# Loading the first token tile whole from the ScalarE queue, and starting the sync queue with w1

## The chip, the cores and the metric

The kernel runs on one core of one Trainium2 chip. The metric is device time in microseconds (us) of one execution, as the median of several. A profile shows one execution, and times in it count from its first instruction. The profiled span is about 2.3 us shorter than the device time of the same execution (547.7 against 549.95 us for the kernel before). In profile lines PE is TensorE, PEld its weight loads, DVE VectorE, ACT ScalarE, POOL GpSimd and SP the sync engine; a q behind the name means the part of the engine that issues DMAs and waits. A load has landed when its completion counter says that all its data have arrived.

## The reference

The reference normalises 2048 tokens of 512 features, runs sliding-window attention with 32 query heads over the last 512 cached keys, runs an MLP on the same normalised tokens, and gates one with the other.

```python
x = A_x
xn = _layernorm(x, axis=-1)
s = _A_ref(xn, A_k_cache, A_v_cache, A_wq, A_wo)   # attention, then wo
g = _silu(_B_ref(xn, B_w1, B_w2))                  # h = silu(xn @ w1); h @ w2
return x + s * g
# x: 1x2048x512, w1: 512x1792, wq: 512x4096, all bf16
```

## The kernel before

The tokens are worked on in four blocks of 512 (four tiles of 128). Only the very start matters for this change. The first block of x and the weights of the MLP are loaded from two queues. `nc.sync` is the queue of the sync engine (SPq in the profile), `nc.scalar` that of ScalarE (ACTq).

```python
new_x(0)
x0v = x2[ds(0, BLK), :].rearrange("(j p) d -> p j d", p=P)
nc.sync.dma_start(x_blk[0][0:HP4, 0, :], x0v[0:HP4, 0, :])      # tile 0, rows 0-63
nc.scalar.dma_start(x_blk[0][HP4:P, 0, :], x0v[HP4:P, 0, :])    # tile 0, rows 64-127
nc.scalar.dma_start(x_blk[0][:, 1, :], x0v[:, 1, :])            # tile 1
NE = NEARLY * P
nc.sync.dma_start(w1_sb[0][:, :, 0 : NE // 2], ...)             # w1, first piece, 256 KB
nc.sync.dma_start(w1_sb[0][:, :, NE // 2 : NE], ...)            # w1, second piece, 256 KB
nc.scalar.dma_start(x_blk[0][:, 2:4, :], x0v[:, 2:4, :])        # tiles 2 and 3
nc.sync.dma_start(w1_sb[0][:, :, NE:], ...)                     # w1, third piece, 384 KB
nc.sync.dma_start(w1_sb[1][:, :, 0:NE], ...)                    # w1, fourth piece, 512 KB
# ... (the rest of w1, w2, later x blocks, keys, wq, values: all on nc.sync)
```

The compute that waits for these loads:

```python
stats(0, 0)                 # VectorE, tile 0
stats(0, 1)                 # VectorE, tile 1, in front of tile 0's centering
for j in range(2):
    rstd_first(j)           # ScalarE
    center(0, j)            # VectorE
warm_up(10)                 # TensorE: matmuls nobody reads
# ... tiles 0 and 1 are transposed on TensorE (t_ps) and copied into xnT
for i in range(2 * FH):
    h_pair(i, i // FH)      # TensorE: h_ps <- xnT (256 tokens) and w1
    if i == 3:
        # ... tiles 2 and 3 are transposed here
```

The last act of the kernel is the output's last pieces, each a store on the sync queue:

```python
for t in range(2):
    # ... last matmuls, two VectorE operations
    nc.sync.dma_start(out2[ds(base // HQ * BLK + (2 + t) * P, P), HALF:], xo)
```

The softmax here doesn't subtract the row's maximum and nothing guards it: scores larger than these inputs give would overflow.

## Time and profile before

| | before |
|---|---|
| median of 3 runs | 550.09 us (549.88 to 551.0) |
| span of the profiled execution | 547.7 us |
| TensorE busy | 542.2 us (99%) |
| first h matmul starts | 6.58 us |
| last matmul starts | 543.59 us |

The busy table of the page and its chain of waits say that TensorE is the limit:

```profile
PE 542.2 (99%) x2676; PEld 261.1 (48%) x2676; DVE 458.4 (84%) x1258; ACT 392.1 (72%) x1125; POOL 20.5 (4%) x41
...
PE 98%; DMA 1%; SPq 0%; DVE 0%; issue 0%
```

The timeline of the first 10 us has, in each line, start, duration, engine, source line, operation, what it writes and reads, and in brackets the idle time in front of it and what ended that:

```profile
0.73 0.55 ACTq L619 DMA_DIRECT2D x_119<-in_A_x_dram  x1
0.73 0.58 SPq L618 DMA_DIRECT2D x_119<-in_A_x_dram  x1
...
1.32 0.60 ACTq L620 DMA_DIRECT2D x_119<-in_A_x_dram  x1
1.37 0.81 SPq L622 DMA_DIRECT2D w_0_111<-in_B_w_dram  x1
...
3.29 0.69 DVE L109 BATCH_NORM_STATS2 st<-x_119 128x6 f32<-128x512 bf16 x1 [2.15 <-DMA x_119<-in_A_x_dram]
...
4.12 0.66 DVE L109 BATCH_NORM_STATS2 st<-x_119 128x6 f32<-128x512 bf16 x1
...
6.58 1.99 PE L691 MATMUL h_ps<-xnT_107,w_0_111 128*128 128x256 bf16 x16
...
8.72 1.48 PE L691 MATMUL h_ps<-xnT_107,w_0_111 128*128 128x256 bf16 x12 [0.16 <-DMA w_0_111<-in_B_w_dram]
...
10.23 0.33 PEld L691 LDWEIGHTS <-w_1_112 128*128 128x128 bf16 x4 [0.30 <-DMA w_1_112<-in_B_w_dram]
```

Read the two statistics first. Tile 0's (3.29) waits for a load; tile 1's (4.12) has no bracket, so tile 1 was there in time. TensorE then starts h at 6.58 and is held up twice by w1, at 8.72 and 10.23. The chain of waits of the same stretch (start, duration, what) names the third piece of w1:

```profile
2.78 5.90 DMA w_0_111<-in_B_w_dram
8.68 0.05 issue
8.72 1.48 PE h_ps L691 x12
```

From the completion counts of the DMAs in the trace come the landings: tile 0's halves 2.84 and 3.20, tile 1 3.79, w1's four pieces 6.32, 7.47, 8.68 and 10.18 us.

The table by stretches shows that the DMA engines were not full at this time; its last two columns are their busy share and GB/s (the share can read a little over 1):

```profile
3.50:4.00 0.50, 0.50 (x2) 0.15 (x1) 0.49 (x1) 0.21 (x1) 0.00 (x0) 1.00 0.41 98
4.00:4.50 0.50, 0.50 (x2) 0.15 (x1) 0.48 (x2) 0.26 (x1) 0.00 (x0) 1.00 0.58 162
```

The last matmul starts at 543.59, the last store is issued at 544.81, and the span ends at 547.68. In between, the sync engine works through a closing list of ten semaphore waits, eight of them one for each completion counter of the DMAs of its own and of ScalarE's queue. Two views, restricted to the sync engine, show it. First, what it waited for after 540 us (total, times, longest):

```profile
SPq L852 <- DMA out_dram<-x_t: 1.1, 1, 1.1
```

Second, its closing instructions between 546.365 and 546.85 us, that is from the landing of the last store on:

```profile
L852 SPq EVENT_SEMAPHORE  x8: 27/28/28, 546.4 to 546.8; - x8
```

So the third wait of the list is the one that waits 1.1 us for the last store. It ends at 546.37, and seven waits still come after it, one every 0.06 us, though nothing is left to wait for.

### The profile page before, as it was taken

The page shows a single profiled execution, that of the slowest core. Times are in us where ns is not written, and L with a number is a line of the kernel's source. Part 1 is how long each engine was busy: PE and PEld are TensorE (multiplying, and loading weights), DVE is VectorE, ACT ScalarE, POOL GpSimd, SP SyncE. Part 2 cuts the span into 40 slices and gives each one's busy share as a digit, 9 for nine tenths or more (in the row PEclk, how much of TensorE's full clock was granted, in tenths as well). Part 3 has the DMA queues.
Part 4 walks back from the last instruction along what each step waited for, and adds up shares of the span by engine and source line. Part 5 has one row for each costly group of instructions (what it writes and reads, how often), then busy time and mean ns, then how long its engine had stood idle before and what let it go on. Part 6 is the DMA issues. An engine that isn't in the chain of part 4 may idle for free.

```text
span 547.7 us, 8533 instructions
## 1 busy us (share of the span) xinstructions
PE 542.2 (99%) x2676; PEld 261.1 (48%) x2676; DVE 458.4 (84%) x1258; ACT 392.1 (72%) x1125; POOL 20.5 (4%) x41
## 2 busy tenths in 40 slices
PE   8999999999999999999999999999999999999997
PEld 5644444444444444444444444444444444444586
DVE  6888888887886788898889888988889889988897
ACT  5558757866875677777777777777788888888600
POOL 1000010000000000010001000100010000000010
PEclk9999999999999999999999999999999999999999
DMA  8969769778849799979887988798889778888921
GB/s 260 278 115 186 160 131 165 152 152 159 168 89 193 171 199 226 211 154 193 160 152 145 189 163 143 155 187 161 145 161 183 153 152 156 185 153 154 173 78 40
DMA packets 298909, 89.69 MB, mean 164 GB/s; under 512 B 282352, under 2 KB 297968, under 8 KB 298864
## 3 DMA queue, kind: packets, MB, share of 16 engines
q1 hardware_dynamic: 297056, 85.02, 79.2%
q0 software_dynamic: 1312, 3.67, 2.6%
q10 hardware_dynamic: 496, 0.46, 0.3%
q8 instruction: 21, 0.34, 0.2%
q14 instruction: 24, 0.20, 0.1%
HBM read 17.30 MB, written 2.10 MB: 35 GB/s over the span
## 4 chain that ended last, share of the span: by engine, by line
PE 98%; DMA 1%; SPq 0%; DVE 0%; issue 0%
PE o_ps L277 20%; PE q_ps L212 20%; PE sc_ps L234 20%; PE s_ps L335 15%; PE oB_ps L181 9%; PE h_ps L148 7%; PE m_ps L478 4%; PE h_ps L691 2%; DMA w_0_111<-in_B_w_dram 1%; SPq L622 0%; SPq L618 0%; SPq L623 0%; PE t_ps L658 0%; DVE m_4_6595 L502 0%; DVE x_t L604 0%
## 5 line engine op out<-in xcount | busy, mean ns | idle before, releaser
L237 ACT ACTIVATE p_all<-sc_ps 128x512 bf16<-128x512 f32 x512 | 305.1, 597 | 104.4 <-PE sc_ps L234 100.4
L249 DVE TENSOR_SCALAR p_all<-p_all,rden 128x512 bf16<-128x512 bf16 x512 | 158.0, 351 | 9.1
L283 DVE CAST oT<-o_ps 128x512 bf16<-128x512 f32 x128 | 88.2, 689 | 35.8 <-PE o_ps L277 35.0
L237 ACT ACTIVATION_READ_ACCUMULATOR p_all<-sc_ps 128x1 f32 x512 | 100.4, 196 | 0.0
L224 DVE CAST qT<-q_ps 128x512 bf16<-128x512 f32 x111 | 76.3, 687 | 3.3 <-PE q_ps L212 3.3
L234 PEld LDWEIGHTS <-qT 128*128 128x128 bf16 x512 | 50.1, 98 | 60.5 <-issue 0.2
L335 PEld LDWEIGHTS <-oT 128*128 128x128 bf16 x384 | 37.6, 98 | 45.3
L247 DVE RECIPROCAL rden<-den 128x2 f32<-128x2 f32 x256 | 40.5, 158 | 11.1 <-ACT p_all L237 10.9
L158 ACT ACTIVATE th<-h_ps 128x512 bf16<-128x512 f32 x42 | 25.0, 595 | 4.0 <-PE h_ps L148 3.9
L335 PE MATMUL s_ps<-wo_big_2344,oT 128*128 128x512 bf16 x84 | 26.0, 379 | 0.0
L335 PE MATMUL s_ps<-wo_big_2084,oT 128*128 128x512 bf16 x84 | 26.0, 379 | 0.0
L335 PE MATMUL s_ps<-wo_big_2345,oT 128*128 128x512 bf16 x84 | 26.0, 379 | 0.0
L335 PE MATMUL s_ps<-wo_big_2083,oT 128*128 128x512 bf16 x84 | 26.0, 379 | 0.0
L234 PE MATMUL sc_ps<-kT_91,qT 128*128 128x512 bf16 x64 | 24.3, 379 | 0.0
L234 PE MATMUL sc_ps<-kT_93,qT 128*128 128x512 bf16 x64 | 24.3, 379 | 0.0
L234 PE MATMUL sc_ps<-kT_95,qT 128*128 128x512 bf16 x64 | 24.3, 379 | 0.0
L234 PE MATMUL sc_ps<-kT_94,qT 128*128 128x512 bf16 x64 | 24.3, 379 | 0.0
L234 PE MATMUL sc_ps<-kT_96,qT 128*128 128x512 bf16 x64 | 24.3, 379 | 0.0
L234 PE MATMUL sc_ps<-kT_97,qT 128*128 128x512 bf16 x64 | 24.3, 379 | 0.0
L234 PE MATMUL sc_ps<-kT_92,qT 128*128 128x512 bf16 x64 | 24.3, 379 | 0.0
L234 PE MATMUL sc_ps<-kT_98,qT 128*128 128x512 bf16 x64 | 23.9, 379 | 0.0
L277 PE MATMUL o_ps<-pT,v_100 128*128 128x512 bf16 x64 | 18.4, 379 | 0.0
(316 smaller groups left out, 858.4 us busy)
## 6 DMA issues: line engine op xcount, KB each, us to landing
pT<-p_all SPq DMA_TRANSPOSE x128, 4.4
x_e<-in_A_x_dram POOLq DMA_DIRECT2D x12, 128.0 KB, 3.2
out_dram<-x_e POOLq DMA_DIRECT2D x12, 128.0 KB, 2.3
w_0_113<-in_B_w_dram SPq DMA_DIRECT2D x1, 896.0 KB, 8.9
w_1_114<-in_B_w_dram SPq DMA_DIRECT2D x1, 896.0 KB, 9.8
w_0_111<-in_B_w_dram SPq DMA_DIRECT2D x2, 256.0 KB, 5.1
w_1_112<-in_B_w_dram SPq DMA_DIRECT2D x1, 512.0 KB, 6.9
x_130<-in_A_x_dram SPq DMA_DIRECT2D x1, 512.0 KB, 8.8
```

What stands on the lines that cost most here:

```text
L148: nc.tensor.matmul(h_ps[:, lo : lo + n], w1_sb[f // FH][:, c, (f % FH) * P : (f % FH + 1) * P], xnT[b][:, c, lo : lo + n], start=(c == 0), ...
L158: nc.scalar.activation(th, h_ps, ACT.Tanh, scale=0.5)
L181: nc.tensor.matmul(cur["ps"], hT[b][f // 2][:, f % 2, j * P : (j + 1) * P], w2_sb[f // FH][:, f % FH, :], start=(f == 0), stop=(f == NFC - 1),
L212: nc.tensor.matmul(cur["ps"], wq_sb[h // REP][:, c, (h % REP) * DH : (h % REP + 1) * DH], xnT[b][:, c, :], start=(c == 0), stop=(c == ND - 1),
L224: nc.vector.tensor_copy(qT[s], cur["ps"])
L234: nc.tensor.matmul(sc, qT[s][:, j * P : (j + 1) * P], kT[h // REP], start=True, stop=True)
L237: nc.scalar.activation(p_all[s][:, :, j, :], sc.rearrange("p (kc q) -> p kc q", q=P), ACT.Exp, scale=INV_SQRT_DH, accum_out=den[s][:, j : ...
L247: nc.vector.reciprocal(rden, den[s][:, j0 : j1 + 1])
L249: nc.vector.tensor_scalar_mul(p_all[s][:, :, j, :], p_all[s][:, :, j, :], rden[:, j - j0 : j - j0 + 1])
L277: nc.tensor.matmul(cur["ps"], v_sb[h // REP][:, kc, :], pT[s][:, kc, :], start=(kc == 0), stop=(kc == NKC - 1))
L283: nc.vector.tensor_copy(oT[s // 2][:, s % 2, :], cur["ps"])
L335: nc.tensor.matmul(acc[j], oT[(b * HQ + h) // 2][:, h % 2, j * P : (j + 1) * P], wo_of(h), start=(h == 0), stop=(h == HQ - 1),)
```

## The change

The intent is to let the sync queue begin with w1, which TensorE is seen waiting for, and to load tile 0 with one load instead of two half ones. The diff has every changed line; context lines are left out:

```diff
@@ -52,7 +52,6 @@
     FH = NFC // 2
     HALF = BLK // 2
     HP = HQ // 2
-    HP4 = P // 2
 
@@ -615,8 +614,7 @@
         new_x(0)
         x0v = x2[ds(0, BLK), :].rearrange("(j p) d -> p j d", p=P)
-        nc.sync.dma_start(x_blk[0][0:HP4, 0, :], x0v[0:HP4, 0, :])
-        nc.scalar.dma_start(x_blk[0][HP4:P, 0, :], x0v[HP4:P, 0, :])
+        nc.scalar.dma_start(x_blk[0][:, 0, :], x0v[:, 0, :])
         nc.scalar.dma_start(x_blk[0][:, 1, :], x0v[:, 1, :])
         NE = NEARLY * P
         nc.sync.dma_start(w1_sb[0][:, :, 0 : NE // 2], w1v[:, :, 0 : NE // 2])
```

## The prediction

> What bounds it now. TensorE is busy 99% of the 547.7 us span (busy table) and is 98% of the chain of waits; granted clock 1.00. After about 11 us it has no gap that matters. So the change can only pay or cost in the first 11 us, and what it moves there passes nearly one to one to the end.
>
> Start-up before (timeline, and DMA completion events of the trace):
> - x tile 0's lower half (sync queue) and upper half (ScalarE queue) are issued at 0.73 us; the ScalarE half lands at 2.84, the sync half at 3.20. Statistics start at 3.29, transposes at 5.35, the last xnT copy ends near 6.55, the first h matmul starts at 6.58. Tile 1 lands at 3.79; VectorE takes it at 4.12 (0.3 us of slack).
> - w1's first piece is issued at 1.37, behind the half tile, and lands at 6.32; pieces two and three at 7.47 and 8.68, the first piece of w1's other half at 10.18. TensorE loses about 0.31 us at 8.72 and 0.18 us at 10.23: 0.5 us that w1 causes.
> - The DMA share by half microseconds is 0.41 and 0.58 from 3.5 to 4.5 us and over 1.0 (near 340 GB/s) only afterwards. An earlier w1 fills an idle hole.
>
> What the change does. It removes one issue from the sync queue: 0.58 us and a 0.06 us step, so w1 is issued 0.64 us earlier (0.73). The ScalarE queue keeps three issues, the first with 128 packets instead of 64. No compute instruction changes; bytes are the same. The Trainium skill ("DMA: Bandwidth & Descriptors", Rules for kernel authors) advises one 128-partition transfer instead of two to disjoint halves, as both use the same 16 engines; the trace agrees so far that the halves land 0.36 us apart, the sync queue's last.
>
> Costed:
> 1. x tile 0 whole on the ScalarE queue: first packet near 2.08, 8 packets of about 50 ns per engine, interleaved with w1's of 27 ns: about 0.65 us, plus 0.3 us to completion: 3.0 to 3.3 (estimate), as now. Tile 1 lands at 3.6 to 4.0. The x chain moves by -0.2 to +0.2 us; I take -0.05.
> 2. w1: first packet near 2.35 instead of 3.0. Landings 0.3 to 0.6 us earlier, less than 0.64 because x shares the engines and the stream is saturated from 4.5 us on.
> 3. TensorE's gaps of 0.31 and 0.18 us shrink: -0.35 us.
> 4. At 18.0 us the first q needs wq's first group, which lands at 17.6 and moves earlier with the stream: no new wait.
>
> Sum: about -0.4 us, 0.07%, below the scatter of the times (549.88 to 551.0).
>
> Predicted: 549.7 us, 8 in 10 between 549.1 and 550.7. Faster by over 2%: 0.003; within 2%: 0.994; slower by over 2%: 0.003.
>
> Right if the profile shows: w1's first issue at 0.73, landing near 5.8; statistics starting at 3.1 to 3.4; first h matmul within 0.2 us of 6.58; waits of the h weight loads for w1 down from 0.9 + 0.3 us to under 0.6; the q group of 18.1 starting near 17.7; everything after shifted, not changed.
>
> Wrong if: the 512 packets of w1's first piece, now beside x's, hold up tile 0 or 1 (a descriptor path shared by both queues would do it): then tile 1's statistics start after 4.3, h after 6.8, and the gain becomes a loss of up to 1 us. Or if tiles 2 and 3, which land at 6.60 just when VectorE wants them (6.62), come later: their transposes at 10.7 would hold TensorE. Or if w1 is limited by the memory and not by its issue: then nothing moves.

## The result and the profile after

| | before | after |
|---|---|---|
| median, 6 runs each | 550.04 us (549.84 to 551.0) | 549.6 us (549.49 to 549.63) |
| ratio of means, 95% interval | | 0.999 (0.9977 to 1.0002) |
| span of the profiled execution | 547.7 us | 547.3 us |
| w1's first piece lands | 6.32 us | 4.17 us |
| tile 1 lands | 3.79 us | 4.57 us |
| first h matmul starts | 6.58 us | 7.19 us |
| 29th h matmul starts (the first that reads w1's fourth piece) | 10.23 us | 10.24 us |
| last matmul starts | 543.59 us | 543.60 us |
| from there to the end (the tail) | 4.09 us | 3.66 us |

A ratio is the mean time of one kernel's fast runs over the mean of the other's in the same rounds, so it is not quite the ratio of the medians. The 0.44 us between the medians is 0.08%. The interval includes 1, because one run of before took 551.0; the six runs of each do not overlap (549.63 at most against 549.84 at least).

The predicted time, 549.7 us, was right to 0.1 us. The table says that the reason was not: TensorE's last matmul starts at the same time in both kernels, and the whole difference of the spans lies behind it. The page is otherwise unchanged:

```profile
PE 542.3 (99%) x2676; PEld 261.5 (48%) x2676; DVE 458.3 (84%) x1258; ACT 392.2 (72%) x1125; POOL 20.5 (4%) x41
...
PE 98%; DMA 1%; DVE 0%; ACTq 0%; ACT 0%; issue 0%
```

The timeline after, of the same stretch:

```profile
0.73 0.43 ACTq L617 DMA_DIRECT2D x_119<-in_A_x_dram  x1
0.73 0.45 SPq L620 DMA_DIRECT2D w_0_111<-in_B_w_dram  x1
...
1.19 0.46 ACTq L618 DMA_DIRECT2D x_119<-in_A_x_dram  x1
1.23 0.51 SPq L621 DMA_DIRECT2D w_0_111<-in_B_w_dram  x1
...
3.33 0.69 DVE L108 BATCH_NORM_STATS2 st<-x_119 128x6 f32<-128x512 bf16 x1 [2.18 <-DMA x_119<-in_A_x_dram]
...
4.59 0.69 DVE L108 BATCH_NORM_STATS2 st<-x_119 128x6 f32<-128x512 bf16 x1 [0.36 <-DMA x_119<-in_A_x_dram]
...
7.19 3.22 PE L689 MATMUL h_ps<-xnT_107,w_0_111 128*128 128x256 bf16 x28
...
10.24 0.60 PE L689 MATMUL h_ps<-xnT_107,w_1_112 128*128 128x256 bf16 x4
```

Tile 1's statistics now have a bracket: they wait for tile 1, although it was issued earlier than before (1.19 against 1.32). Everything behind them is late, and h starts 0.61 us later. But then 28 matmuls run in one piece: the waits for w1 are gone. The chain of waits names tile 1's load where it named w1's:

```profile
1.19 3.38 DMA x_119<-in_A_x_dram
4.57 0.02 issue
4.59 0.70 DVE st L108
...
7.19 3.65 PE h_ps L689 x32
```

The idle hole of the DMA engines is filled, as was hoped:

```profile
3.50:4.00 0.50, 0.50 (x3) 0.15 (x1) 0.50 (x1) 0.00 (x0) 0.00 (x0) 1.00 1.11 365
4.00:4.50 0.50, 0.50 (x2) 0.15 (x1) 0.20 (x2) 0.23 (x1) 0.00 (x0) 1.00 1.14 346
```

At the end, the same two views of the sync engine (the second from 546.365 to 546.43 us):

```profile
SPq L850 <- DMA out_dram<-x_t: 0.6, 1, 0.6
```

```profile
L850 SPq EVENT_SEMAPHORE  x1: 28/28/28, 546.4 to 546.4; - x1
```

The last store lands at the same time as before. But the wait for it is now the last of the list; the other nine were done while the store was still under way. Seven waits of 0.06 us are 0.43 us; the tail is shorter by 4.09 - 3.66 = 0.43 us, and the spans differ by 0.42.

Why the position moved can be read in the compiled programs. The loads and stores of the two hardware queues take eight completion counters in turn (they are called DMAHW0 to DMAHW7 there), and the closing list asks for them in the order of their numbers. Before a counter is taken again, its previous use is waited for, so the last store's line tells its counter:

```
before: DMACopy out_dram<-x_t 128x256 [waits DMAHW0_49,DVE_49]
after:  DMACopy out_dram<-x_t 128x256 [waits DMAHW7_49,DVE_49]
```

The change removes one load at the start. That shifts every later load and store by one counter, and the last one from the first counter to the last. The traces agree: the last store of before uses the same counter that the third closing wait asks for, that of after the counter of the tenth.

### The profile page after: what moved, and what is told of

It is laid out like the page before. It is cut to its first block, busy times and chain, and to the rows that moved or that the text cites. A ratio compares the mean times of both kernels' runs of the same rounds, so it can differ in the third digit from the quotient of the medians.

```text
span 547.3 us, 8530 instructions
## 1 busy us (share of the span) xinstructions
PE 542.3 (99%) x2676; PEld 261.5 (48%) x2676; DVE 458.3 (84%) x1258; ACT 392.2 (72%) x1125; POOL 20.5 (4%) x41
## 4 chain that ended last, share of the span: by engine, by line
PE 98%; DMA 1%; DVE 0%; ACTq 0%; ACT 0%; issue 0%
PE sc_ps L233 20%; PE q_ps L211 20%; PE o_ps L276 20%; PE s_ps L334 15%; PE oB_ps L180 9%; PE h_ps L147 7%; PE m_ps L477 4%; PE h_ps L689 2%; DMA x_119<-in_A_x_dram 1%; DVE st L108 0%; PE t_ps L647 0%; PE t_ps L656 0%; DVE m_4_6594 L501 0%; ACTq L617 0%; DVE x_t L603 0%; ACT xnT_107 L651 0%
## 5 line engine op out<-in xcount | busy, mean ns | idle before, releaser
L351 POOL DMA_DIRECT2D out_dram<-x_e x12 | 6.6, 550 | 314.7 <-DVE rden L246 258.4
```

## The experiments

Two questions were open. Does the gain come from the tail (theory T) or from w1's head start (theory S, my prediction)? And why did tile 1 come late, so that the start-up gained nothing?

Medians of before in these rounds: 550.08 us (11 or 12 runs, 549.71 to 552.27), and 550.13 in the last two experiments. The long runs of before pull its mean up, and with it the ratios down a little.

### The changed kernel, with the last store back on the first counter

```diff
         for s in range(NSTEP):
             b, h = divmod(s, HQ)
+            if s in (70,):
+                pad = const.tile([16, 16], BF16, name=f"pad{s}", tag=f"pad{s}")
+                nc.sync.dma_start(pad, x2[0:16, 0:16])
```

> The changed kernel with one 512-byte load more on the sync queue, in mid-kernel (step 70), so the sync and ScalarE queues issue as many DMAs as in the kernel before and the last output store uses the first of the eight completion counters again. Theory T (tail): the 0.44 us come from the closing waits of the sync engine alone; undone here: ratio to before 1.000 (550.0 us), seven waits of 0.06 us after the last store has landed, end 4.1 us after the last matmul begins; the start-up stays as in the changed kernel. Theory S (start-up, as predicted): the gain is w1's 0.64 us head start; it stays: 549.6 us, ratio 0.9992.

Measured: 549.92 us (549.73 to 550.25), ratio 0.9994 (0.9981 to 1.0006). The tail is back at 4.08 us; between the last store's landing and 547.15 us the sync engine has eight closing waits again, the one that waited and seven more:

```profile
L853 SPq EVENT_SEMAPHORE  x8: 28/28/28, 546.7 to 547.1; - x8
```

A 512-byte load in mid-kernel, which nothing reads, took back about 0.3 of the 0.44 us in the medians, and all of the tail in the trace. The start-up of this trace also differed from the changed kernel's first one: tiles 2 and 3 landed at 7.41 instead of 6.90 us, TensorE waited to transpose them, and the last matmul started at 543.89. So the time by itself speaks for T but not sharply; the tail does. The wait:

```profile
10.77 0.72 PE L656 MATMUL t_ps<-ident,x 128*128 128x128 bf16 x8 [0.24 <-DVE x L123]
```

### The kernel before, with the last store on the last counter

```diff
+            if s in (70, 71, 72, 73, 74, 75, 76):
+                pad = const.tile([16, 16], BF16, name=f"pad{s}", tag=f"pad{s}")
+                nc.sync.dma_start(pad, x2[0:16, 0:16])
```

> The kernel before with seven 512-byte loads more on the sync queue (steps 70 to 76), so that the last output store uses the last of the eight counters, as in the changed kernel. Start-up untouched. T: 0.42 us faster than before, 549.6 us, ratio 0.9992; one wait left after the last store has landed, end 3.66 us after the last matmul begins. S: no gain, ratio 1.000 or a little slower for the seven loads.

Measured: 549.55 us (549.48 to 550.03), ratio 0.9987 (0.9975 to 1.0). The tail is 3.66 us, the last matmul starts at 543.57, and the start-up is that of before (first h matmul 6.79, 29th 10.22). What the sync engine waited for, and its one closing wait after the landing (546.355 to 546.42 us):

```profile
SPq L855 <- DMA out_dram<-x_t: 0.6, 1, 0.6
```

```profile
L855 SPq EVENT_SEMAPHORE  x1: 28/28/28, 546.4 to 546.4; - x1
```

So the whole time of the changed kernel is had without the change, by seven useless loads. T holds and S falls. This run also isolates the start-up: with the same tail, the changed kernel (549.60, and 549.67 when repeated) is not faster than this kernel with before's start-up (549.55); the runs are of different rounds.

### w1 held back by one small load

The rest of the experiments ask about the start. The first one puts a small load in front of w1.

```diff
+        pad = const.tile([16, 16], BF16, name="pad")
+        nc.sync.dma_start(pad, x2[0:16, 0:16])
         nc.scalar.dma_start(x_blk[0][:, 0, :], x0v[:, 0, :])
         nc.scalar.dma_start(x_blk[0][:, 1, :], x0v[:, 1, :])
```

> The changed kernel with a 512-byte load as the first issue of the sync queue, so w1 is issued about 0.6 us later, near its old time, and x tile 0 stays whole on the ScalarE queue; as many DMAs as before. Theory C (w1's packets, now on the engines before tile 1's, hold tile 1 up by 0.8 us, and that loss takes back w1's gain): tile 1 lands before 4.2 us, the first h matmul starts near 6.6, and the h weight loads wait for w1 again; start-up as a whole as before, and with the tail of before 550.0 us, ratio 1.000. Rival (the 128-packet first tile itself delays tile 1 in its own queue): tile 1 still lands near 4.6 and h starts near 7.2, with w1 later too: 550.2 or more.

Measured: 550.09 us (549.93 to 550.57), ratio 0.9998 (0.9985 to 1.0012). The time is as theory C said, but its mechanism failed: tile 1 landed at 4.63, and h started at 7.14. The trace shows that the experiment was badly dosed. The small load's issue took 0.40 us, not the 0.6 that I had assumed from the half tile's, so w1 was issued at 1.19, 0.02 us after tile 1. The packets of the two were then sent mixed. It tells nothing between C and its rival, which names tile 0 in tile 1's own queue as the cause.

### Tile 1 at the head of the sync queue

```diff
-        nc.scalar.dma_start(x_blk[0][:, 1, :], x0v[:, 1, :])
+        nc.sync.dma_start(x_blk[0][:, 1, :], x0v[:, 1, :])
```

> The changed kernel with x tile 1 moved to the head of the sync queue, in front of w1; as many DMAs as in the changed kernel, so its tail. C: tiles 0 and 1 land by 3.4 us, the first h matmul starts near 6.5, w1's pieces land with less than 0.3 us of waits: 0.3 to 0.5 us faster than the changed kernel, near 549.2 us, ratio to before 0.9984. If w1 is limited by bytes ahead of it: its waits return, h starts at 6.5 but TensorE reaches the transposes at 10.7 as before: 549.6 us.

Measured: 549.26 us (549.0 to 549.87), ratio 0.9983 (0.997 to 0.9996). The timeline:

```profile
3.56 0.69 DVE L108 BATCH_NORM_STATS2 st<-x 128x6 f32<-128x512 bf16 x1 [2.42 <-DMA x<-in_A_x_dram]
...
4.38 0.66 DVE L108 BATCH_NORM_STATS2 st<-x 128x6 f32<-128x512 bf16 x1
...
6.84 3.71 PE L689 MATMUL h_ps<-xnT,w 128*128 128x256 bf16 x32
```

Tile 1 is no longer waited for. Tile 1 landed at 3.37 and tile 0 at 3.53, a little later than the 3.4 expected, and h started at 6.84, not 6.5. Tiles 2 and 3 landed at 5.47 instead of 6.90. But h then ran through 32 matmuls with hardly a wait for w1, and the last matmul started at 543.30 us, 0.30 earlier than in the changed kernel. In this trace the head start that was to be gained is there; one trace alone does not prove it, as a later section shows. With the tail of the changed kernel its median is below both.

### w1 held back by two small loads

```diff
+        for i in range(2):
+            pad = const.tile([16, 16], BF16, name=f"pad{i}", tag=f"pad{i}")
+            nc.sync.dma_start(pad, x2[0:16, 0:16])
         nc.scalar.dma_start(x_blk[0][:, 0, :], x0v[:, 0, :])
```

> The changed kernel with two 512-byte loads at the head of the sync queue (the earlier hold had one, and w1 was then issued 0.02 us after tile 1, too close to tell). w1's first piece is now issued near 1.6 us, clearly after tile 1 (near 1.2). Theory D (the loads of the two queues are turned into packets one whole load at a time, in the order of issue, so tile 1 waits for w1's 512 packets when w1 was issued first or at the same time): tile 1 lands by 3.9 us, its statistics follow tile 0's without a wait for the load, the first h matmul starts by 6.6. Rival (tile 1 waits for tile 0 in its own queue): tile 1 lands near 4.6 as in the changed kernel and h starts near 7.2. Tail by T: the last store uses the second counter, so one closing wait fewer than before comes after it: 4.03 us from the start of the last matmul to the end against 4.09.

Measured: 549.65 us (549.31 to 549.86), ratio 0.9987 (0.9973 to 1.0001).

```profile
1.17 0.46 ACTq L621 DMA_DIRECT2D x<-in_A_x_dram  x1
1.64 0.42 SPq L623 DMA_DIRECT2D w<-in_B_w_dram  x1
...
3.81 0.66 DVE L108 BATCH_NORM_STATS2 st<-x 128x6 f32<-128x512 bf16 x1
...
6.57 2.33 PE L692 MATMUL h_ps<-xnT,w 128*128 128x256 bf16 x17 [0.44 <-DMA w<-in_B_w_dram]
```

Tile 1, issued 0.02 us earlier than in the changed kernel and behind the same whole tile 0 in the same queue, landed at 3.38 instead of 4.57 us. Apart from the two small loads, only w1 had moved, to 1.64. So it is w1 in front of it, on the other queue, that holds tile 1 up, and the rival falls. The packets in the trace say how. Packets begun in each quarter of a microsecond (w1's are 512 bytes, the tiles' 1 KB):

```
                        2.25 2.50 2.75 3.00 3.25 3.50 3.75 4.00
after  ScalarE queue      34   47    7    0   13   75   39    1   (to 2.99: tile 0; from 3.25: tile 1)
after  sync queue, w1      1   34  134  169  145   34   94  169
two    ScalarE queue      84   53   53    2    1    1    6   17   (to 3.24: tiles 0, 1; then tiles 2 and 3)
loads  sync queue, w1      0    0   26   40   25    8   29   68
```

In the changed kernel the ScalarE queue falls silent between tile 0 and tile 1 while w1's first piece is sent, and the sync queue drops while tile 1 is sent. So these loads took turns nearly as wholes, in the order of issue: tile 1, 128 packets, stood behind w1's 512. This is not shown as a rule. In the first hold, with issues 0.02 us apart, the packets mixed. In the kernel before, tiles 2 and 3 were issued 0.58 us after w1's first piece, and yet 53 of their packets and 62 of w1's were begun in the quarter from 4.75 us. The counts add up all DMA engines, so whether a single engine took the loads in turn is not told.

The price is seen in the last line of the timeline: h now starts at 6.57 with a wait for w1, whose first piece landed only at 6.53. The last matmul started at 543.49. The tail was 4.04 us with the last store on the second counter, 0.05 less than on the first, where one wait of 0.06 was expected.

### Tile 0 split by columns instead of rows

In the kernel before, the first issues were long (0.55 to 0.60, and 0.81 for w1's first piece, against 0.43 to 0.46 after). This asks whether loads of 64 partitions make them so.

```diff
-        nc.sync.dma_start(x_blk[0][0:HP4, 0, :], x0v[0:HP4, 0, :])
-        nc.scalar.dma_start(x_blk[0][HP4:P, 0, :], x0v[HP4:P, 0, :])
+        DH2 = D // 2
+        nc.sync.dma_start(x_blk[0][:, 0, 0:DH2], x0v[:, 0, 0:DH2])
+        nc.scalar.dma_start(x_blk[0][:, 0, DH2:], x0v[:, 0, DH2:])
```

> The kernel before with tile 0 split by columns instead of rows: two loads of 128 partitions x 256 columns, one on each queue; the same bytes, as many DMAs, the same order. Theory H (loads of 64 partitions are what made the first issues of the kernel before long and w1's first piece slow): first issues under 0.5 us instead of 0.56 to 0.60, w1's first piece's issue under 0.55 instead of 0.81, and its landing before 5.4 instead of 6.32. Rival (any split over two queues costs it): issues stay near 0.6 and 0.8, w1's first piece lands after 6. Time between 549.6 and 550.3 in either case.

Measured: 550.24 us (549.94 to 552.09), ratio 1.0003 (0.9987 to 1.0019). The halves were issued in 0.39 and 0.41 us, w1's first piece in 0.42, and it landed at 5.17: theory H on all three. But its landing is not due to the shape alone: with 64-partition loads absent too, w1 landed at 6.53 in the experiment with two small loads, where it stood behind tile 1. Here w1 was issued 0.02 us after tile 1, the two were sent mixed as in the first hold, tile 1 landed at 4.89 and h started at 7.41. Tile 0 itself landed no later than before (2.83 and 2.99 against 2.84 and 3.20), so I put the late tile 1 down to the closer issue; no experiment tested that apart.

### The two kernels once more

> The changed kernel once more, unaltered, for a second trace. T: end 3.66 us after the start of the last matmul again, 549.6 us. Start-up: tile 1's statistics wait for its load again (start after 4.3) and the 29th h matmul starts at 10.2 (within 0.1 us of before).

> The kernel before once more, unaltered, for a second trace. T: end 4.09 us after the start of the last matmul. Start-up: w1's first piece lands after 6 us and the 29th h matmul starts at 10.2 again.

Measured: the changed kernel 549.67 us (549.48 to 549.67), tail 3.66, tile 1's statistics at 4.51, 29th h matmul at 10.05, last matmul 543.65. The kernel before, one run of 549.63 us: tail 4.09, w1's first piece at 6.38, but the 29th h matmul at 9.83 and the last matmul at 543.18, where 10.2 was expected. So the start-up of one and the same kernel scatters by 0.4 us between executions, here by w1's fourth piece (9.79 against 10.18). That the two first traces agreed to 0.01 us at the 29th matmul was a coincidence; that the change gains nothing there rests on the experiment with seven loads, not on these traces.

The traces show a second loss that the change brought. In the three with the changed start-up (after, its repetition, after with one load more) tiles 2 and 3 landed at 6.90, 7.17 and 7.41 us; in the three with that of before at 6.60, 6.23 and 6.55. w1's second piece, issued at 1.23 us in after, now lands in front of them (5.45); in before it was issued and landed behind them (2.24, 7.47). From the 29th to the 33rd h matmul, between which tiles 2 and 3 are transposed, TensorE took 0.88, 1.03 and 1.39 us against 0.89 in each of the other three. So in two of three traces a part of what w1 gained was lost here.

### The best version again, and a further step

The version with tile 1 on the sync queue was run again unaltered, and with tiles 2 and 3 moved to the sync queue as well:

```diff
-        nc.scalar.dma_start(x_blk[0][:, 1, :], x0v[:, 1, :])
+        nc.sync.dma_start(x_blk[0][:, 1, :], x0v[:, 1, :])
         # ... w1, first and second piece
-        nc.scalar.dma_start(x_blk[0][:, 2:4, :], x0v[:, 2:4, :])
+        nc.sync.dma_start(x_blk[0][:, 2:4, :], x0v[:, 2:4, :])
```

> The version with tile 1 at the head of the sync queue once more, unaltered. C: again 549.2 to 549.4 us, some 0.3 us faster than the changed kernel, no wait for tile 1's load, first h matmul near 6.8, the 29th near 9.9. If the first result was chance: 549.6.

> As that version, and tiles 2 and 3 moved to the sync queue too, behind w1's second piece; the ScalarE queue issues tile 0 alone. D (loads are turned into packets in the order of issue): w1's first two pieces get in front of tiles 2 and 3 and land earlier (first piece by 4.8 instead of 5.4), tiles 2 and 3 land by 6.6. As h then waits for tiles 0 and 1 alone, and w1's fourth piece still has the same bytes in front of it: 549.0 to 549.4 us. If tiles 2 and 3 land after 6.8, VectorE waits for them and it is slower, 549.5 or more.

Measured: the repetition 549.1 us (549.01 to 549.48), ratio 0.997 (0.9952 to 0.9988), so the gain over before, tail included, is no chance. Against the changed kernel there are only runs of different rounds: nine of the 12 runs of this version lie below all ten of the changed kernel (549.48 to 549.67). (Its profile fell on its slowest run, 549.48, with h at 7.12: the tiles were there as early, at 3.33 and 3.50, but the first four transposes on TensorE took 0.61 us instead of 0.40. Why is open.) The further step 549.53 us (549.4 to 549.89), ratio 0.9979 (0.9963 to 0.9996): w1's first piece landed at 4.78 as expected of the order of issue, but tiles 2 and 3 at 7.46, not by 6.6, and VectorE waited for them:

```profile
7.49 0.69 DVE L108 BATCH_NORM_STATS2 st<-x 128x6 f32<-128x512 bf16 x1 [0.29 <-DMA x<-in_A_x_dram]
```

In the medians it lost again what the previous step had gained. How much of that is this wait the trace does not settle: it fell on the slowest run (549.89), the stretch from the 29th to the 33rd h matmul was 0.22 us longer than in the previous step, and the first transposes were slow here too (0.61 us).

All versions, sorted by the counter of the last store:

| version | median us | last store's counter | tail in the profile, us | last matmul starts, us |
|---|---|---|---|---|
| before | 550.04 | first | 4.09 | 543.59 and 543.18 |
| after, one load more | 549.92 | first | 4.08 | 543.89 |
| one small load before w1 | 550.09 | first | 4.09 | 543.55 |
| columns | 550.24 | first | 4.07 | 543.81 |
| two small loads before w1 | 549.65 | second | 4.04 | 543.49 |
| after | 549.60 and 549.67 | last | 3.66 | 543.60 and 543.65 |
| before, seven loads more | 549.55 | last | 3.66 | 543.57 |
| tile 1 on sync | 549.26 and 549.10 | last | 3.66 | 543.30 and 543.53 |
| tiles 1, 2, 3 on sync | 549.53 | last | 3.66 | 543.95 |

## Why the prediction was right, and where its reasons were not

The number was right (549.7 predicted, 549.6 measured, about 0.4 us faster). Its account of the 0.4 us was wrong, so that the number came out was luck: a gain at the end that I had not looked for had the size of the one that I expected at the start.

- "What bounds it now": right. TensorE is busy 99% in both, and what its first 11 us gain or lose reappears in the start of the last matmul: from the 33rd h matmul (11.12 us in both) to the last one it is 532.46 to 532.57 us in both and in all the other traces.
- "w1 is issued 0.64 us earlier (0.73)": right, 0.73.
- Step 1, "Tile 1 lands at 3.6 to 4.0. The x chain moves by -0.2 to +0.2 us": this is the step that failed. Tile 0 landed at 3.30, in the range, but tile 1 at 4.57 and h started at 7.19, +0.61 us. I had let w1's packets and x's alternate on the engines. The loads took turns nearly as wholes, and tile 1 came behind w1's first piece. The prediction's own list of what would make it wrong names this and its signs (statistics of tile 1 after 4.3, h after 6.8); both came. So did its next item, that tiles 2 and 3 come later and hold TensorE: in two of three traces.
- Step 2, "Landings 0.3 to 0.6 us earlier": mis-sized. w1's four pieces landed 2.15, 2.02, 1.02 and 1.00 us earlier (6.32 to 4.17, 7.47 to 5.45, 8.68 to 7.66, 10.18 to 9.18). The earlier issue is 0.64 of it; being in front of tile 1 instead of behind it fits the rest: with tile 1 at the head of the sync queue, w1's first piece was issued 0.45 us later than in the changed kernel and landed 1.23 us later (5.40).
- Step 3, "-0.35 us": the waits did go, even altogether. But they were spent on the late start: h runs from 6.58 to 10.84 before and from 7.19 to 10.84 after. Net gain at the last matmul: none in these two traces (543.59, 543.60), and none in the times of the seven-load experiment.
- Step 4, no new wait at the first q: right, but it did not start near 17.7; it started at 18.11 in both.
- What was not in the prediction at all: removing one load moves the last store from the first to the last of eight completion counters, and the closing list of waits, 0.06 us each, is then worked off before the last store lands instead of after it. That is 0.42 us of the 0.44, shown in the tail by undoing it (after, one load more) and in tail and time by doing it alone (before, seven loads more).

The Trainium skill, "DMA: Bandwidth & Descriptors", "Issuing engines are not separate DMA queues", says that DMAs from different engines end up on the same 16 DMA engines and interleave. The first point fits this trace: in the quarter from 3.50 us, in which tile 1 sends 75 packets, w1 drops from 145 to 34. The interleaving was coarser than I took it for: in the quarter from 3.00 us tile 1, issued at 1.19, sent no packet while w1 sent 169.

What stays open: where the turns are decided (the descriptors' making or the engines themselves), and why w1's first piece, when it stands behind tile 1, is not only later but slower (in before its packets left the engines at a share of 0.41 from 3.5 to 4.0 us, with w1 alone under way). The two-load experiment shows the same slow stretch without any 64-partition load (0.38 in the same half microsecond), so the half tiles are not needed for it; in both, though, loads over fewer than 128 partitions stood in front of w1 on its queue.

## What to carry to other kernels

When a change adds or removes a DMA, look at the end of the trace too: where the last store's completion stands in the closing waits can be worth more than the change itself, and it can be had by another change in the number of DMAs that puts the last store on the same counter. When two queues start together, order the loads by who is waited for first over both queues, not in each: a big load that is issued first, even on the other queue, can go first nearly as a whole (here with 0.46 us between the issues). And a predicted time that comes out right proves nothing about its reasons until the place of the gain has been found in the trace.

## What the Trainium skill lacked or had wrong

- "DMA: Bandwidth & Descriptors", "Issuing engines are not separate DMA queues": neither this section nor "Queues, rings and completion order" on the same page, which treats the switching between queues, says that the order of issue over two queues can decide which load is sent first, nearly as a whole. Measured here: tile 1 (128 KB) issued at 1.17 to 1.19 us landed at 4.57 with a 256 KB load issued at 0.73 on the other queue, and at 3.38 with that load issued at 1.64.
- The same page, "Rules for kernel authors": the advice to use one 128-partition load for two disjoint halves gives as reason that both use the same engines. It does not speak of the issues, which were also longer here with halves by rows: 0.55 and 0.58 us against 0.41 and 0.39 with halves by columns, and 0.81 against 0.42 for w1's issue just behind them.
- No page that I looked up speaks of the closing waits on the completion counters: eight counters, about 0.06 us each, and 0.43 us between a last store on the first and on the last of them. "Runtime: NRT & Kernel Launch", "The ~15µs preamble/postamble breakdown", lists for the end a barrier for all engines to be done and the resetting of semaphores and DMA rings, but no such list.
